# Splitting the next head's q and k at the head of a step, and a two-bank PSUM tile with a place of its own

## The chip, the cores and the metric

The kernel runs on one NeuronCore of one Trainium2 chip. The metric is the device time of one execution in microseconds (us). The engines named below are TensorE (PE in the rows, with its weight loads as PEld), VectorE (DVE), ScalarE (ACT), GpSimd (POOL) and SyncE (SP, which issues the DMAs here).

## What is computed

Causal attention with a monotone bias over 32 heads (4 x 8), 576 positions, 64 columns a head, then two MoE-like blocks on the 2304 tokens:

```python
scores = where(causal, -1e9, scale * q @ k.T + minimum(bias, 0))   # bias from a cumsum of max(s, 0)
x = softmax(scores) @ v                     # heads laid side by side: 2304 x 512
h = (x @ w1) * (x @ w2) @ w3                # 512 -> 1024 -> 1024
x = h @ w_out                               # 1024 -> 512
h = x @ w_in                                # 512 -> 1024
sm = softmax(h); solu = h * sm
ln = (solu - mean) / sqrt(var + 1e-6) * g_ln
out = ln @ w_out2                           # 1024 -> 512
```

## The kernel before

Most products are made from a high and a low word of each operand: ScalarE copies the operand into the rounded type (`hi`), an engine subtracts that from the operand (`lo`), and TensorE adds three products, high by high, high by low and low by high. The order of all instructions is set by a scheduler that goes through the program text and by the pools: an instruction waits for the buffer that its tile takes, and a tile takes the buffer that comes free first in its pool.

**Attention.** A loop over steps `st` (36 of them) issues for one head its scores (`qk_part`, parts 0 to 2: matmuls `sc`, lines 177 and 178, VectorE's masked maximum on line 186, ScalarE's exponential on line 190) and for the head two steps earlier the transposes (`tr`, line 247) and the products with v (`av`, line 275). The first 8 heads use unsplit q and k. From head 8 on `split_qk` splits them: ScalarE's `hi` of 64 x 1152 (line 93), a DMA that copies it (line 159), and GpSimd's `lo` (line 98). A step's head is split in the step before it, behind the transposes of that step.

Between these stand the units of the first MoE block as filler (`ab_unit`): 12 matmuls `a` = x·w1 (line 303), ScalarE's copy to `a_sb` (line 315), 12 matmuls `b` = x·w2, VectorE's product `g_sb` (line 323), which goes to DRAM (`g_scr`).

**Weights.** `pump` prepares weights, one job of 512 KB at a time. A job's DMA brings packed words into a `stage` buffer (2 buffers in the attention, 4 after it); ScalarE (line 340) and VectorE (lines 346, 347, 351) turn them into fp32; ScalarE makes the high word `W` (line 93) and VectorE the low word (line 98). The low word frees the stage buffer for the next DMA. 16 of these jobs, for w1 and w2, run in steps 3 to 16, beside the first units.

**PSUM.** It has eight banks. Up to step 10 a pool psA holds two tiles of two banks (`bigtile`, for the 576 columns of scores of a head's longest rows, the first matmul of part 0) and psB four of one bank (`smalltile`, for all the rest). At step 11 both are closed and replaced by psE, one tile of two banks, and psF, six of one bank. The first score tile of head 9 is the first that psE gives.

**M.** After the attention 16 jobs bring w3, and `m_unit(f)` makes the eight row blocks of M = w3·w_out (24 matmuls of 128x512, line 626). Its bank is a `smalltile`. The first comes right behind the last unit's `b`; the others follow in psD, four one-bank tiles of the pools that replace psE and psF. Then `x2_half` (`x`, line 710) multiplies g by M, `h_pair` computes h by seven products of halves in four banks with the tags X, Y, Z, W (psC), the softmax and the layer norm follow, and `out_unit(t)` computes the output tile of 128 rows: 24 matmuls of 128x512 (line 836), ScalarE's copy (line 841) and one DMA of 256 KB (line 842). There are 18 such tiles, and the last is the program's end.

Of the kernel before, what the change touches and what calls it, by code (L numbers as in the profile page):

```python
# [8 lines left out]
F32 = mybir.dt.float32  # L9
# [3 lines left out]
AF = mybir.ActivationFunctionType  # L13
ALU = mybir.AluOpType
AX = mybir.AxisListType
PSUM = bass.MemoryType.PSUM
# [10 lines left out]
def tile_attention_moe(  # L27
# [15 lines left out]
    nc = tc.nc  # L43
    B, H, D, _, S = qkT.shape
    NH = B * H
    T, DM = out.shape
# [3 lines left out]
    KF = DF // 128  # L50
# [6 lines left out]
    for i in (2, 3, 1, 4, 0):  # L57
# [3 lines left out]

    dram = ctx.enter_context(tc.tile_pool(name="dram", bufs=1, space=DRAM))
    ps_ctx = ExitStack()
    PSP = [
        ps_ctx.enter_context(tc.tile_pool(name="psA", bufs=2, space=PSUM)),
        ps_ctx.enter_context(tc.tile_pool(name="psB", bufs=4, space=PSUM)),
# [15 lines left out]
    def bigtile(name):  # L82
        return PSP[0].tile([128, 2, 512], F32, tag="A", name=name)

    def smalltile(name):
        return PSP[1].tile([128, 512], F32, tag="B", name=name)

    def flat(ap):
        return ap.rearrange("p a b -> p (a b)")
# [34 lines left out]
    def load_head(h):  # L124
        b, hh = divmod(h, H)
        if h < NQ:
            nc.sync.dma_start(out=QN[h % 3][64:128], in_=qkT[b, hh, :, 0])
            after[0] = nc.sync.dma_start(out=KN[h % 3][64:128], in_=qkT[b, hh, :, 1])
            return
        qk2 = at.tile([128, 2, S], F32, tag="qk2", bufs=2, name="qk2")  # L130
        after[0] = nc.sync.dma_start(
            out=qk2[64:128].rearrange("p a s -> p (a s)"), in_=qkT[b, hh].rearrange("d a s -> d (a s)"),
        )
        raw_t[h] = qk2[64:128]
# [18 lines left out]
    def split_qk(h):  # L153
        if h < NQ:
            return
        raw = raw_t.pop(h)
        t = QK[h % 2]
        hi(t[64:128, 0::2], raw)
        nc.sync.dma_start(out=t[0:64, 1:3].bitcast(F32), in_=t[64:128, 0::2].bitcast(F32))
        lo(t[64:128, 1::2], raw, t[64:128, 0::2], G)  # L160
# [36 lines left out]
    def qk_part(h, part):  # L197
        if part == 0:
            p_t[h] = at.tile([128, PW], F32, tag="P", bufs=PB, name="P")
        if part == 0:  # L200
            ps = flat(bigtile("sc"))
            qk_mm(h, [(0, ps[:, 512:1024]), (512, ps[:, 448:512])], 0)
            softmax_tile(h, 0, ps[:, 448:1024])
            return
        ps = smalltile("sc")
        o = 0
        views = []
        for ti in ((1, 4), (2, 3))[part - 1]:
            q0, rows, n, _ = QT[ti]
            qk_mm(h, [(0, ps[:, o:o + n])], ti)  # L210
            views.append((ti, ps[0:rows, o:o + n]))
            o += n
        for ti, view in views:
            softmax_tile(h, ti, view)
# [277 lines left out]
    for i in range(2):  # L492
# [14 lines left out]
        out=wmask[:, S - 128:S], in_=wmask[:, S - 128:S], pattern=[[-1, 128]],  # L507
# [36 lines left out]
    for st, (h, ph) in enumerate(steps):  # L544
        for _ in range(NF.get(st, 0)):
            fill.extend(ab_unit(*units.pop(0)))
        left = len(fill)
        if st == 11:
            ps_ctx.close()
            PSP[:] = [  # L550
                ps_ctx.enter_context(tc.tile_pool(name="psE", bufs=1, space=PSUM)),
                ps_ctx.enter_context(tc.tile_pool(name="psF", bufs=6, space=PSUM)),
            ]

        def F(share):
            while fill and len(fill) > left * (1 - share):
                fill.pop(0)()

        if h is not None:
            if NQ <= h + 2 < NH:  # L560
                load_head(h + 2)
            qk_part(h, 0)
        if st > 1:
            pump(PUMP.get(st, 0))
        if h is not None:
            qk_part(h, 1)
            qk_part(h, 2)
        F(FS)
        if h is not None:
            normalise(h)  # L570
        if ph is not None:
            for part in range(4):
                tr_part(ph, part)
        if late:
            with tc.issue_after(last_tr[0].ins):
                for fn in late.pop():
                    fn()
        if h is not None:
            if h % 2 == 1:
                load_v(h // 2)  # L580
            if NQ - 2 <= h < NQ:
                t = QK[h % 2] = at.tile([128, 4, S], F32R, tag="QK", bufs=2, name=f"QK{h % 2}")
                aug_rows(t[:, 0], t[:, 3])
            if h + 1 < NH:
                split_qk(h + 1)
            if h + 3 < NQ:
                load_head(h + 3)
                load_aug(h + 3, cumf_scr[h + 3:h + 4])
            if NQ <= h + 2 < NH:
                load_aug(h + 2, cum_scr[h + 2])  # L590
        F(1)
        if ph is not None and ph % 2:
            parts = av_parts(ph // 2)
            if ph < PD or st == len(steps) - 1:
                for fn in parts:
                    fn()
            else:
                late.append(parts)
# [4 lines left out]
    NT = T // 128  # L603
# [15 lines left out]
        w_job(w3L[f, :, 1024 * i:1024 * i + 1024], dst)  # L619

    def m_unit(f):
        ps = smalltile("m")
        for k in range(KF):
            H3, L3 = m_st[f, k // 4]
            for w_, o_ in ((H3, WOH), (H3, WOL), (L3, WOH)):
                nc.tensor.matmul(
                    ps, w_[:, k % 4], o_[:, k],
                    start=(k == 0 and w_ is H3 and o_ is WOH), stop=(k == KF - 1 and w_ is L3),
                )
        hi(MH[:, f], ps)  # L630
        lo(ML[:, f], ps, MH[:, f])
# [8 lines left out]
    for i in range(8):  # L640
# [8 lines left out]
    behind.clear()  # L649
    right0.close()  # L650
    ps_ctx.close()
    PSP[:] = [
        ctx.enter_context(tc.tile_pool(name="psC", bufs=1, space=PSUM)),
        ctx.enter_context(tc.tile_pool(name="psD", bufs=4, space=PSUM)),
    ]
    HD = DF // 2

    r2 = ctx.enter_context(tc.tile_pool(name="r2", bufs=1, side="right"))
# [39 lines left out]
    def x2_half(c, i):  # L698
        ps = smalltile("x2").rearrange("p (a t) -> p a t", a=2)
        x2_t[c, i] = ps  # L700
        last = None
        for a in range(2):
            m = 2 * i + a
            with ExitStack() as order:
                if last is not None:
                    order.enter_context(tc.issue_after(last.ins))
                for k in range(KF):
                    GH, GL = g_hl[c][k // 2]
                    for w_, g_ in ((MH, GH), (MH, GL), (ML, GH)):
                        last = nc.tensor.matmul(  # L710
                            ps[:, a], w_[:, k, m * 128:m * 128 + 128], g_[:, k % 2],
                            start=(k == 0 and w_ is MH and g_ is GH), stop=(k == KF - 1 and w_ is ML),
                        )
        if i == 1:
            g_hl.pop(c)
# [114 lines left out]

    def out_unit(t):
        LH, LL = lt_t.pop(t)
        ps = smalltile("o")
        for k in range(KF):
            for l_, w_ in ((LH, OH), (LH, OL), (LL, OH)):
                nc.tensor.matmul(  # L836
                    ps, l_[:, k], w_[:, k],
                    start=(k == 0 and l_ is LH and w_ is OH), stop=(k == KF - 1 and l_ is LL),
                )
        o = p2.tile([128, DM], F32, tag="o", bufs=1, name="o")  # L840
        nc.scalar.activation(out=o, in_=ps, func=AF.Copy)
        nc.sync.dma_start(out=out[t * 128:t * 128 + 128], in_=o)

    NCH = NT // 2

    def h_pair(c):
        t0, t1 = 2 * c, 2 * c + 1
        for t in (t0, t1):
            so = p2.tile([128, DF], F32, tag="so", bufs=2, name="so")
            ln_t[t] = so, p2.tile([128, 8], F32, tag="sv", bufs=4, name="sv")  # L850
        h0, h1 = ln_t[t0][0], ln_t[t1][0]
        X, Y, Z, W = (PSP[0].tile([128, HD], F32, tag=n, name=f"h{n}") for n in "XYZW")
        h_mm(X, "A11", "B11", True)
        copy(h0[:, 0:HD], X)
        h_mm(Z, "S1", "T1", True)
        copy(h1[:, HD:], Z)
        h_mm(Y, "A12", "B21", True)
        meet(t0, 0, Y)
        h_mm(X, "S2", "T2", False)
        copy(h0[:, HD:], X)  # L860
        if c + 1 < NCH:
            x2_first(c + 1)
        h_mm(Z, "S4", "B22", False)
        meet(t0, 1, Z)
        ln_exp(t0)
        h_mm(W, "A22", "T4", True)
        h_mm(X, "S3", "T3", False)
        copy(h1[:, 0:HD], X)
        ln_mean(t0)
        meet(t1, 1, X)  # L870
        meet(t1, 0, W)
        ln_exp(t1)
        ln_apply(t0)
# [34 lines left out]
    p2 = ctx.enter_context(tc.tile_pool(name="p2", bufs=1, side="left"))  # L908
    OH = p2.tile([128, KF, DM], F32R, name="OH")
    OL = p2.tile([128, KF, DM], F32R, name="OL")  # L910
    x2_half(0, 0)
    x2_first(0)
    x2_half(0, 1)
# [7 lines left out]
    for c in range(NCH):  # L921
# [8 lines left out]
        last = c == NCH - 1  # L930
# [77 lines left out]
```

## Time and profile before

| | us |
|---|---|
| median of 3 runs | 732.38 (731.66 to 733.02) |
| the profiled execution, its own time | 732.8 |
| its span, first to last instruction | 731.1 |
| TensorE busy | 714.2 |
| VectorE busy | 507.7 |
| ScalarE busy | 470.4 |
| GpSimd busy | 95.2 |

The span is what the rows cover; 1.7 us of the execution's own time lie outside it. The profiled execution is 0.4 us above the median, inside the range of the runs. A busy TensorE is one that has a matmul in flight; a matmul's row shows from its start to its modelled end, so that rows of consecutive matmuls overlap and the rate is read from their starts.

### The profile page before, as it was taken

The numbers are of one execution on the slowest core, as the hardware profiler recorded it, in microseconds if no ns is written. First come the engines' busy times: TensorE is split into PE (matmuls) and PEld (weight loads), VectorE is DVE, ScalarE is ACT, GpSimd is POOL, SyncE is SP. The second block draws the span as 40 slices with busy tenths as digits, with TensorE's granted clock in tenths as the row PEclk, the third lists the DMA queues.
The fourth block names the chain that finished last, engine by engine and source line by source line (L and its number), as shares of the span: only waits on it lengthen the run. The fifth ranks groups of instructions, "written<-read, shape, count | busy, mean of one in ns | idle before, by whom it ended". The sixth has DMA issues, their size and how long they took to land.

```text
span 731.1 us, 12896 instructions
## 1 busy us (share of the span) xinstructions
PE 714.2 (98%) x4618; PEld 631.5 (86%) x4618; DVE 507.7 (69%) x1251; ACT 470.4 (64%) x977; POOL 95.2 (13%) x88
## 2 busy tenths in 40 slices
PE   9989998999999999999998999999999999999997
PEld 6669888889899999999997889988888988888886
DVE  7996989898777887822777966675747366563651
ACT  7996878798676777822544735576737465563742
POOL 3051322234121221000000000001000000000000
PEclk9999999999999999999999999999999999999999
DMA  5644555555476655514566933153324252302311
GB/s 124 190 135 132 156 164 146 164 148 127 140 205 184 207 164 175 179 62 161 185 204 201 378 114 101 59 116 87 79 66 102 45 133 68 87 19 68 66 36 43
DMA packets 79827, 95.50 MB, mean 131 GB/s; under 512 B 41418, under 2 KB 52682, under 8 KB 79764
## 3 DMA queue, kind: packets, MB, share of 16 engines
q1 hardware_dynamic: 79764, 94.69, 44.5%
q8 instruction: 36, 0.59, 0.3%
q14 instruction: 27, 0.22, 0.1%
HBM read 59.04 MB, written 20.14 MB: 108 GB/s over the span
## 4 chain that ended last, share of the span: by engine, by line
PE 81%; DVE 9%; DMA 5%; ACT 2%; issue 2%; SPq 0%; DVEq 0%; ACTq 0%
PE x L710 14%; PE o L836 14%; PE a L303 12%; PE b L303 11%; PE av L275 6%; PE hX L742 5%; PE tr L247 5%; DMA stage<-in_w_dram 4%; PE hZ L742 3%; PE sc L178 2%; PE sc L177 2%; PE hW L742 2%; PE hY L742 2%; DVE stage L351 2%; PE sc L169 1%
## 5 line engine op out<-in xcount | busy, mean ns | idle before, releaser
L190 ACT ACTIVATE P<-P,STAT 64x64 f32<-64x64 f32 (+4 forms) x160 | 88.5, 556 | 22.9 <-DVE STAT L186 22.3
L98 POOL TENSOR_TENSOR QK<-qk,QK 64x1152 fp32r<-64x1152 f32 x24 | 66.2, 2759 | 172.9 <-ACT QK L93 172.8
L710 PE MATMUL x<-gl,MH 128*128 128x256 f32 x288 | 80.4, 279 | 0.0
L710 PE MATMUL x<-gh,ML 128*128 128x256 f32 x288 | 80.2, 279 | 0.0
L710 PE MATMUL x<-gh,MH 128*128 128x256 f32 x288 | 79.9, 279 | 0.0
L303 PE MATMUL b<-xT0h,W 128*128 128x288 f32 x256 | 58.4, 301 | 3.5 <-DVE W L98 2.1
L303 PE MATMUL a<-xT0h,W 128*128 128x288 f32 x256 | 59.2, 306 | 0.0
L247 PE MATMUL tr<-ident,P 128*128 128x128 f32 x416 | 54.4, 275 | 3.5 <-DVE STAT L186 2.7
L303 PE MATMUL a<-xT1h,W 128*128 128x288 f32 x256 | 57.6, 300 | 0.0
L836 PE MATMUL o<-OH,lh 128*128 128x512 f32 x144 | 57.0, 396 | 0.2 <-DVE ll L98 0.2
L836 PE MATMUL o<-OH,ll 128*128 128x512 f32 x144 | 57.0, 396 | 0.0
L836 PE MATMUL o<-OL,lh 128*128 128x512 f32 x144 | 57.0, 396 | 0.0
L303 PE MATMUL b<-xT1h,W 128*128 128x288 f32 x256 | 56.4, 295 | 0.0
L710 PEld LDWEIGHTS x<-gl,MH 128*128 128x128 f32 x288 | 54.1, 188 | 1.5 <-DVE gl L98 0.2
L710 PEld LDWEIGHTS x<-gh,MH 128*128 128x128 f32 x288 | 53.9, 188 | 1.1
L710 PEld LDWEIGHTS x<-gh,ML 128*128 128x128 f32 x288 | 54.0, 188 | 0.9
L806 DVE COPY lt<-turned 128x2048 uint16<-128x2048 uint16 x16 | 22.0, 1373 | 45.4 <-DMA turned<-half 45.4
L247 PEld LDWEIGHTS tr<-ident,P 128*128 128x128 f32 x416 | 46.8, 141 | 5.4 <-issue 1.6
L323 DVE TENSOR_TENSOR g_sb<-b,a_sb 128x288 f32<-128x288 f32 x64 | 28.7, 450 | 31.6 <-PE b L303 21.5
L340 ACT ACTIVATE stage<-stage 128x512 f32<-128x512 f32 x56 | 37.1, 679 | 20.5 <-DMA stage<-in_w_dram 18.7
L226 ACT ACTIVATE P<-P,STAT 128x576 f32<-128x576 f32 x64 | 42.7, 717 | 10.5 <-DVE STAT L219 10.4
L315 ACT ACTIVATE a_sb<-a 128x288 f32<-128x288 f32 x64 | 25.7, 403 | 36.3 <-PE a L303 36.0
(191 smaller groups left out, 1984.1 us busy)
## 6 DMA issues: line engine op xcount, KB each, us to landing
stage<-in_w_dram SPq DMA_DIRECT2D x32, 512.0 KB
g_scr<-g_sb SPq DMA_DIRECT2D x32, 288.0 KB
stage<-in_wo_dram SPq DMA_DIRECT2D x16, 512.0 KB
qk<-in_qk_dram SPq DMA_DIRECT2D x24, 288.0 KB
QK<-QK SPq DMA_DIRECT2D x24, 288.0 KB
gl<-g_scr SPq DMA_DIRECT2D x24, 256.0 KB
wf<-wf_scr SPq DMA_DIRECT2D x22, 256.0 KB
out_dram<-o SPq DMA_DIRECT2D x18, 256.0 KB
```

The costliest lines, as they stand in the source:

```text
L98: eng.tensor_tensor(out=dst, in0=src, in1=hi_.bitcast(F32), op=ALU.subtract)
L190: ex = nc.scalar.activation(out=dst, in_=dst, func=AF.Exp, bias=st[0:rows, ti:ti + 1], scale=-1.0, accum_out=st[0:rows, 5 + ti:6 + ti],)
L226: nc.scalar.activation(out=dst, in_=src, func=AF.Copy, scale=r)
L247: last_tr[0] = nc.tensor.transpose(ps[:, 128 * n:128 * n + 128], pt[:, o:o + 128], ident)
L275: nc.tensor.matmul(st["ps"][64 * e:64 * e + 64, 448 + c0:448 + c1], vr[:, j, e], PT[(2 * p + e) % 4][:, o + c0:o + c1], **kw,)
L303: nc.tensor.matmul(ps, w_[:, c, fs], x_[:, c, sl], start=(c == 0 and w_ is WH and x_ is XH), stop=(c == KC - 1 and w_ is WL),)
L315: ab_last[0] = nc.scalar.activation(out=a_sb, in_=ps, func=AF.Copy).ins
L323: ab_last[1] = nc.vector.tensor_tensor(out=g[:, sl], in0=ps, in1=st["a"], op=ALU.mult).ins
L340: nc.scalar.activation(out=high.bitcast(F32), in_=high.bitcast(F32), func=AF.Copy, scale=2.0 ** -112)
L710: last = nc.tensor.matmul(ps[:, a], w_[:, k, m * 128:m * 128 + 128], g_[:, k % 2], start=(k == 0 and w_ is MH and g_ is GH), stop=(k == KF ...
L742: last_h[0] = nc.tensor.matmul(ps, x_[:, k], w_[:, k], start=first and k == 0 and x_ is XH and w_ is WH, stop=k == 1 and x_ is XL, skip_gr ...
L836: nc.tensor.matmul(ps, l_[:, k], w_[:, k], start=(k == 0 and l_ is LH and w_ is OH), stop=(k == KF - 1 and l_ is LL),)
```

## The change

Four edits.

1. `split_qk(h + 1)` goes from behind the transposes of a step to the step's head, ahead of `qk_part(h, 0)` and of `pump`.
2. psE, the two-bank tile of step 11, is taken from the right side of PSUM, where psB's banks lay, and stays open past the end of the attention. Before, it lay on the left, where psA's lay.
3. M's first block takes that two-bank tile (its first bank) in place of a one-bank tile of psF. In `h_pair` the tags Z and W keep psC, X and Y get two banks in a new pool psG, which opens where psE lay, once psE is closed.
4. The last output tile is computed in two halves of 256 columns, each with 24 matmuls, a copy and a DMA of 128 KB, the second half's matmuls behind the first's.

```diff
         if st == 11:
             ps_ctx.close()
             PSP[:] = [
-                ps_ctx.enter_context(tc.tile_pool(name="psE", bufs=1, space=PSUM)),
+                big_ctx.enter_context(tc.tile_pool(name="psE", bufs=1, space=PSUM, side="right")),
                 ps_ctx.enter_context(tc.tile_pool(name="psF", bufs=6, space=PSUM)),
             ]
...
         if h is not None:
             if NQ <= h + 2 < NH:
                 load_head(h + 2)
+            if h + 1 < NH:
+                split_qk(h + 1)
             qk_part(h, 0)
...
-            if h + 1 < NH:
-                split_qk(h + 1)
             if h + 3 < NQ:
...
     def m_unit(f):
-        ps = smalltile("m")
+        ps = smalltile("m") if f else bigtile("m")[:, 0]
...
-    PSP[:] = [
-        ctx.enter_context(tc.tile_pool(name="psC", bufs=1, space=PSUM)),
-        ctx.enter_context(tc.tile_pool(name="psD", bufs=4, space=PSUM)),
-    ]
+    psp = {}
+    psp["Z"] = psp["W"] = ctx.enter_context(tc.tile_pool(name="psC", bufs=1, space=PSUM))
+    PSP[1] = ctx.enter_context(tc.tile_pool(name="psD", bufs=4, space=PSUM))
...
-        ps = smalltile("o")
-        for k in range(KF):
...
         o = p2.tile([128, DM], F32, tag="o", bufs=1, name="o")
-        nc.scalar.activation(out=o, in_=ps, func=AF.Copy)
-        nc.sync.dma_start(out=out[t * 128:t * 128 + 128], in_=o)
+        last = None
+        for c0, c1 in ((0, DM),) if t < NT - 1 else ((0, DM // 2), (DM // 2, DM)):
+            ps = smalltile("o")[:, 0:c1 - c0]
...
+            nc.scalar.activation(out=o[:, c0:c1], in_=ps, func=AF.Copy)
+            nc.sync.dma_start(out=out[t * 128:t * 128 + 128, c0:c1], in_=o[:, c0:c1])
...
+    big_ctx.close()
+    psp["X"] = psp["Y"] = ctx.enter_context(tc.tile_pool(name="psG", bufs=1, space=PSUM, side="right"))
```

The order of instructions moves only in some places: between head 9's first scores and the scores of head 15; where M passes into x; in the first `h_pair` calls; and in the last output tile. In all other places each engine has the same rows in the same order.

TensorE, at the first scores of head 9 (`QK_656`, in the change `QK_659`, is that head's split q and k), before:

```order
L303 MATMUL b<-xT0l,W_124 128x288
L303 MATMUL b<-xT0h,W_125 128x288
L177 MATMUL sc<-QK_656 128x512 [waits DMAHW0_49,DMAHW7_49,PE_49,Pool_49]
L178 MATMUL sc<-QK_656 128x512 [waits DMAHW1_49]
L177 MATMUL sc<-QK_656 128x64
L178 MATMUL sc<-QK_656 128x64
L303 MATMUL a<-xT0h,W_122 128x288 [waits Activation_49]
```

and with the change:

```order
L304 MATMUL b<-xT0h,W_124 128x288
L304 MATMUL b<-xT0l,W_124 128x288
L304 MATMUL b<-xT0h,W_125 128x288
L178 MATMUL sc<-QK_659 128x512 [waits DMAHW0_49,DMAHW7_49,DVE_49,Pool_49]
L179 MATMUL sc<-QK_659 128x512 [waits DMAHW1_49]
L178 MATMUL sc<-QK_659 128x64
L179 MATMUL sc<-QK_659 128x64
```

The scores now stand behind one more unit (12 `a` and 12 `b`) than before, and wait for VectorE, which reads the bank of that side last (a `g_sb`), in place of TensorE.

ScalarE, in the step of head 10 (`W02_124` is the high word of one weight job, `W00_122` of the next; `QK0_595` is head 10's split; P and STAT are the exponentials), before:

```order
L93 ACTIVATE QK1_656<-qk2_896 64x2x576
L190 ACTIVATE P_956,STAT2_118<-P_956,STAT2_118 128x576
L93 ACTIVATE W02_124<-stage_758 128x4x128
L93 ACTIVATE QK0_595<-qk2_954 64x2x576
L190 ACTIVATE P_898,STAT1_117<-P_898,STAT1_117 128x448
```

and with the change:

```order
L94 ACTIVATE P_959,STAT2_118<-P_959,STAT2_118 64x64
L94 ACTIVATE QK0_595<-qk2_954 64x2x576
L191 ACTIVATE P_959,STAT2_118<-P_959,STAT2_118 128x320
L316 ACTIVATE a_sb_1014<-a_1001 128x288
L191 ACTIVATE P_959,STAT2_118<-P_959,STAT2_118 128x192
L191 ACTIVATE P_959,STAT2_118<-P_959,STAT2_118 128x576
L94 ACTIVATE W02_124<-stage_761 128x4x128
L94 ACTIVATE W00_122<-stage_769 128x4x128
```

The first high word went behind head 10's split and behind the exponentials of two heads, and stands right ahead of the second.

VectorE, in the step of head 14 (`W_129` is the low word of a job; line 351, in the change 352, is the last step of a job's fp32 words, the one in front of `W_129` before being the next job's), before:

```order
L347 SCALAR_TENSOR_TENSOR stage<-stage 128x512
L228 TENSOR_SCALAR P<-P,STAT_116 64x64
L95 COPY PT_115<-tr 128x512
L95 COPY PT_115<-tr 64x3x64
L351 SCALAR_TENSOR_TENSOR stage<-stage 128x512
L98 TENSOR_TENSOR W_129<-stage,W_128 128x4x128
L186 ISA P,STAT_118<-sc,lmask 128x576
```

and with the change:

```order
L187 ISA P,STAT_118<-sc,lmask 128x576
L187 ISA STAT_118 128x1
L348 SCALAR_TENSOR_TENSOR stage<-stage 128x512
L96 COPY PT_115<-tr 128x128
L229 TENSOR_SCALAR P<-P,STAT_117 128x320
L229 TENSOR_SCALAR P<-P,STAT_117 128x192
L99 TENSOR_TENSOR W_129<-stage,W_128 128x4x128
L352 SCALAR_TENSOR_TENSOR stage<-stage 128x512
```

The low word now stands behind that head's first masked maximum and ahead of the next job's last step.

## Rows read from the trace of the kernel before

**Rows 1.** The page: busy time, share of the span and instructions.

```profile
PE 714.2 (98%) x4618; PEld 631.5 (86%) x4618; DVE 507.7 (69%) x1251; ACT 470.4 (64%) x977; POOL 95.2 (13%) x88
```

**Rows 2.** TensorE's waits from 60 to 160 us: total, times, longest.

```profile
PE b L303 <- DVE W L98: 2.1, 1, 2.1
PE tr L247 <- DVE STAT L186: 1.4, 1, 1.4
PE b L303 <- ACT W L93: 0.8, 1, 0.8
PE b L303 <- DVE g_sb L323: 0.7, 1, 0.7
PE sc L177 <- DVE g_sb L323: 0.3, 1, 0.3
```

**Rows 3.** Windows: PE, PEld, DVE, ACT, POOL busy, PEclk (granted clock), DMA share, GB/s.

```profile
80.00:100.00 20.00, 17.81 (x120) 16.71 (x120) 17.75 (x51) 16.37 (x48) 6.49 (x2) 0.91 0.60 178
120.00:140.00 20.00, 17.38 (x120) 15.64 (x121) 18.09 (x49) 15.08 (x35) 5.17 (x2) 0.91 0.65 187
160.00:350.00 190.00, 190.00 (x1453) 174.10 (x1452) 132.38 (x364) 123.66 (x303) 33.50 (x13) 1.00 0.52 158
```

**Rows 4.** VectorE's timeline from 79 to 124 us: start, duration, what.

```profile
79.97 3.14 DVE L98 TENSOR_TENSOR W<-stage,W 128x512 fp32r<-128x512 f32 x1
...
119.87 0.94 DVE L95 COPY PT<-tr 128x512 f32<-128x512 f32 x2
120.74 2.31 DVE L351 SCALAR_TENSOR_TENSOR stage<-stage 128x512 uint32<-128x512 uint32 x1
122.97 0.68 DVE L98 TENSOR_TENSOR W<-stage,W 128x512 fp32r<-128x512 f32 x1
```

**Rows 5.** GpSimd's timeline at 119 us.

```profile
119.86 2.64 POOL L98 TENSOR_TENSOR QK<-qk,QK 64x1152 fp32r<-64x1152 f32 x1 [5.71 <-ACT QK L93]
```

**Rows 6.** TensorE's timeline at 97 us.

```profile
97.67 0.30 PE L303 MATMUL b<-xT0h,W 128*128 128x288 f32 x1
```

**Rows 7.** ScalarE's timeline at 76 us and at 92 us.

```profile
76.87 0.67 ACT L93 ACTIVATE W<-stage 128x512 fp32r<-128x512 f32 x1
...
92.73 1.16 ACT L93 ACTIVATE QK<-qk 64x1152 fp32r<-64x1152 f32 x1
```

**Rows 8.** The chain of waits from 82 to 98 us: start, duration, what.

```profile
83.14 3.87 DMA stage<-in_w_dram
...
88.09 3.31 DMA stage<-in_w_dram
```

**Rows 9.** TensorE's waits from 380 to 440 us.

```profile
PE m L626 <- DVE g_sb L323: 2.2, 1, 2.2
PE m L626 <- ACT w3h L93: 0.6, 1, 0.6
```

**Rows 10.** The chain of waits from 427 to 429 us.

```profile
427.26 0.69 DVE stage L351
427.98 0.69 ACT w3h L93
```

**Rows 11.** Matmuls of x at 442 us, and the end of the last output tile.

```profile
441.83 0.28 PE L710 MATMUL x<-gl,MH 128*128 128x256 f32 x1
...
442.77 0.28 PE L710 MATMUL x<-gh,MH 128*128 128x256 f32 x1
...
726.68 0.40 PE L836 MATMUL o<-OL,lh 128*128 128x512 f32 x1
726.91 0.40 PE L836 MATMUL o<-OH,ll 128*128 128x512 f32 x1
727.40 0.60 ACT L841 ACTIVATE o<-o 128x512 f32<-128x512 f32 x1 [5.00 <-PE o L836]
```

**Rows 12.** ScalarE's copies of one shape, 60 to 300 us: busy, mean ns.

```profile
L93 ACT ACTIVATE PT<-tr 128x256 f32<-128x256 f32 x21 | 7.8, 372 | 0.0
```

**Rows 13.** DMA traffic from 727 to 731.1 us in 40 slices.

```profile
GB/s 0 0 0 0 0 0 0 0 0 0 0 0 0 0 0 0 0 0 360 380 340 380 380 440 240 40 0 0 0 0 0 0 0 0 0 0 0 0 0 0
```

More of the change, by code (lines that the diff above doesn't have):

```diff
@@ L63, in tile_attention_moe @@
     ps_ctx = ExitStack()
+    big_ctx = ExitStack()
     PSP = [
@@ L832, in out_unit @@
         LH, LL = lt_t.pop(t)
-        ps = smalltile("o")
-        for k in range(KF):
[L835 to L839, printed above, removed]
-        o = p2.tile([128, DM], F32, tag="o", bufs=1, name="o")
-        nc.scalar.activation(out=o, in_=ps, func=AF.Copy)
-        nc.sync.dma_start(out=out[t * 128:t * 128 + 128], in_=o)
+        o = p2.tile([128, DM], F32, tag="o", bufs=1, name="o")
+        last = None
+        for c0, c1 in ((0, DM),) if t < NT - 1 else ((0, DM // 2), (DM // 2, DM)):
+            ps = smalltile("o")[:, 0:c1 - c0]
+            with ExitStack() as order:
+                if last is not None:
+                    order.enter_context(tc.issue_after(last.ins))
+                for k in range(KF):
+                    for l_, w_ in ((LH, OH), (LH, OL), (LL, OH)):
+                        last = nc.tensor.matmul(
+                            ps, l_[:, k], w_[:, k, c0:c1],
+                            start=(k == 0 and l_ is LH and w_ is OH), stop=(k == KF - 1 and l_ is LL),
+                        )
+            nc.scalar.activation(out=o[:, c0:c1], in_=ps, func=AF.Copy)
+            nc.sync.dma_start(out=out[t * 128:t * 128 + 128, c0:c1], in_=o[:, c0:c1])
     NCH = NT // 2
@@ L851, in h_pair @@
         h0, h1 = ln_t[t0][0], ln_t[t1][0]
-        X, Y, Z, W = (PSP[0].tile([128, HD], F32, tag=n, name=f"h{n}") for n in "XYZW")
+        X, Y, Z, W = (psp[n].tile([128, HD], F32, tag=n, name=f"h{n}") for n in "XYZW")
         h_mm(X, "A11", "B11", True)
```

## Prediction, on record before the change was run

> **What bounds the kernel now.** I read the page first: TensorE has a matmul in flight in 98% of the span [rows 1], so a gain must come out of the 2% in which it has none, out of a lower clock, or out of the two ends of the program. The list of TensorE's waits says where the idle time lies: five waits between 60 and 160 us, 0.3 + 0.7 + 1.4 + 0.8 + 2.1 = 5.3 us [rows 2], and two at M, 2.2 and 0.6 us [rows 9]. The windows then show two things that the waits don't. From 160 to 350 us TensorE is busy for 190.00 of 190 us [rows 3], though heads are split there too, so the split as such costs nothing in that stretch. And in two windows, 80 to 100 and 120 to 140 us, the mean granted clock is 0.91 [rows 3]. As the clock has two levels, 1.2 and 2.4 GHz, 0.09 x 20 us = 1.8 us of full-speed work is lost in each. Each fall follows an idle spell of TensorE, of 1.4 us in the first window and of 0.8 and 2.1 us in the second. So the stretch from 70 to 130 us holds 5.3 + 2 x 1.8 = 8.9 us that could come back at most.
>
> The timelines name the causes. At 121.6 us a `b` unit waits for a low word `W`. VectorE stood in the next job's line 351, which took 2.31 us in place of 0.69 [rows 4, 10], and only then made the low word; GpSimd's `lo` of a head's q and k ran from 119.86 for 2.64 us [rows 5], the time in which that instruction was slow. At 79.97 us a low word itself took 3.14 us against the usual 0.68 [rows 4]; that one freed a stage buffer late, its DMA started at 83.14, the next job's at 88.09 and landed 3.31 us later, at 91.40 [rows 8], and VectorE stood at line 346 for it, ahead of a masked maximum that the transposes at 91 us waited for (the 1.4 us).
>
> **The change, part by part.** The trace shows none of the new order, so I walk it through: each instruction begins when its engine is free and what it waits for is done, with the duration of its row before.
>
> *PSUM tile on the right, split at the head (edits 1 and 2).* The same instructions run, in another order, from head 9's scores to head 15's.
> - Start: head 9's scores now wait for the third unit's `g_sb`, right behind that unit's last `b`. Such waits took 0.3 and 0.7 us [rows 2]; I give the new one 0.6 in place of the 0.3: +0.3.
> - The high word that ended at 77.5 us [rows 7] now stands behind head 10's split and the exponentials of heads 9 and 10. In the walk it comes at some 83.5. Its low word follows at 84 to 85, and the next job's at 86. So the stage loads start at some 84.7 and 86 in place of 83.14 and 88.09 [rows 8]; the first is late by 1.6 us, the second early by 2. By 3.3 to 3.9 us a load, stretched as two now run together, they land at about 89 and 91. What is late next is the following `b` unit, whose high word stands on ScalarE behind head 12's split, its exponentials and two copies: about 96.9. In the trace before that unit starts at 97.67 [rows 6], at half clock. So here the new order is 0.7 us ahead, the +0.3 counted in.
> - Around 120 us: the low word stands ahead of the next job's line 351, and the matmuls that need it stand later. In the walk the high word is ready at about 119, as TensorE gets there, and the low word at about 122, where TensorE needs it at 122.8. The waits of 0.8 and 2.1 us go, and with them the clock's fall: -4.7.
>
> That would be -5.4 at 130 us. Behind it the order is as before and TensorE has no wait to 350 us [rows 3], so what is gained there stays. But the walk takes every VectorE instruction at its usual length. GpSimd's `lo` is moved, not removed, and some VectorE instruction will run beside it. I take off one stretched low word, 3.14 - 0.68 = 2.46 [rows 4], and count -2.9. The bounds are -5.4 (nothing stretched that TensorE waits for; -8.9 if no other wait is left either) and the slower rival below. The split's ScalarE copy and its DMA are issued as often as before. On SP's queue the stage loads now stand behind the split's DMA and behind the next load of q and k, which waits for GpSimd's `lo` to free its buffer; in the walk GpSimd is done at about 84, just ahead of the low word that lets the stage load go, so I give this 0, and it would cost a `b` unit what GpSimd is later.
>
> The Trainium skill, GPSIMD Engine Reference, section Key points, says that GpSimd shares its SBUF interfaces with VectorE and that VectorE instructions with two SBUF inputs contend for them. The trace agrees: two copies out of PSUM took 0.94 us together beside the same GpSimd instruction that stretched line 351, which has two SBUF inputs, to 2.31 [rows 4, 5]. The rule speaks against the edit, since a move leaves the contention: by the rule alone the term would be near the upper end, by the walk alone -5.4.
>
> *M's first block in the two-bank tile (edit 3).* The first `m` waits 2.2 us for the last `g_sb` because it gets that product's bank [rows 9]. The two-bank tile is free since the last head's scores, and w_out's words and the first of w3's are made by then, or the wait would be for them; the wait goes. But M's blocks are fed by a chain of DMA, VectorE and ScalarE work that doesn't start from TensorE here: the words for a late block come at 427.98 + 0.69 = 428.67 us whatever TensorE does, where it waits 0.6 us already [rows 9, 10]. A TensorE that is 2.2 us earlier waits 2.8 there. What is left is the chain's own gain: VectorE's order has that job's line 351 (427.26 before [rows 10]) one instruction earlier, 0.6 us. I take -0.6; the ends are 0 and -2.2 (the chain moves up by all of it, as blocks that are read out earlier hold VectorE less).
>
> *psC and psG.* The same number of banks and users; TensorE has no wait in `h_pair`, and the changed order of the first pairs lies under its matmuls: 0. If a tag had to wait for psG's opening, it would cost at most one `h` product; I see no such wait in the order.
>
> *The last tile in halves (edit 4).* 48 matmuls of 256 columns for 24 of 512. By starts, x's 256 columns come each 0.94 / 8 = 0.118 us, and the output's 512 each 0.23 [rows 11]: 48 x 0.118 = 5.6 against 24 x 0.23 = 5.5, so 0 to +0.1. Behind the last matmul, the copy falls from 0.60 us [rows 11] to about the 0.37 of another copy of 128x256 [rows 12]: -0.23. The last DMA moves half: its bytes took 7 to 8 slices of 0.1 us [rows 13], so -0.35. The first half's copy and DMA lie under the second half's 2.8 us of matmuls. Together -0.5, between -0.2 (only the copy) and -0.6.
>
> Sum: -2.9 - 0.6 + 0 - 0.5 = -4.0 us. The profiled execution took 732.8, so 728.8; that execution lies 0.4 above the median, so I forecast 728.4 for the median.
>
> **The rivals.**
> - *All of it comes back.* No stretched instruction meets a low word that TensorE waits for, and M's chain moves up: -5.4 - 2.2 - 0.6 = -8.2, so 724.2. For it: the walk. Against it: VectorE is busy for 17.8 to 18.1 of 20 us there [rows 3], so little slack is left for any delay.
> - *The stalls only move.* The loads come no earlier in sum, a `b` unit still waits 2 to 3 us for its words, and the clock falls once more: the attention gives between 0 and -1, with M and the end 730.3 to 731.9. For it: the same work on the same full engines, 16 jobs through two stage buffers. Against it: the two waits before have named causes, and both causes are gone in the order.
> - *Slower: GpSimd's `lo` meets the low word at 97 us.* In the walk the high word there ends at 96.9, with no slack to the `b` that needs it, and the low word follows at once. GpSimd takes 2.64 us [rows 5]; if the head's split on ScalarE ends after 96.9 - 2.6 = 94.3 us, the low word runs beside it and takes 2.46 us longer, TensorE waits, and the clock falls as behind the other waits: 2.46 + 1.8 = 4.3. The next stage load leaves as much later, so that the wait around 120 us stays too. Then -0.7 + 4.3 - 0.6 - 0.5 = +2.5, so 734.9. For it: the split of that step ended at 92.73 + 1.16 = 93.9 before [rows 7], 0.4 us from there, and the walk's errors are of this size. Against it: the change issues the split ahead of what it stood behind.
>
> **How the numbers follow.** The forecast, within 1.8 us either way (726.6 to 730.2): 0.45. All comes back: 0.15. The stalls only move: 0.24. Slower: 0.16. The 80% range leaves out most of the slower case and the far end of the best one: 724.5 to 733.3. A measurement of this kernel tells 0.2%, 1.5 us, from no change, so faster means below 730.9. That takes the first two cases and a third of the third, 0.67; the rest of the third and a little of the slower one make 0.18 for the same; slower 0.15.
>
> **What the profile of the changed kernel would show.** Right: no wait of TensorE for a `W` low word over 1 us between 110 and 130 us, a granted clock of 1.0 in that window, the first `m` right behind the last `b`, a longer wait of `m` for `w3h` at M's end (some 2 us), and an end in which the last copy takes 0.37 us. Wrong: a `W` of line 99 that takes 2 us or more with a `b` behind it, a clock below 1 in a window from 80 to 130 us, or a gain at M that outlasts the last block. What would make the forecast wrong most is the first stretch, as its term is a difference of waits that each hang on half a microsecond.

## The result: 1% slower, and the profile after

| | us |
|---|---|
| before, median | 732.38 |
| the change, median of 5 runs | 740.08 (738.83 to 741.04) |
| ratio to before | 1.0098, 95% interval 1.0079 to 1.0118 |
| the change's profiled execution: its time, its span | 738.83, 737.1 |

The change is 7.2 us slower by the ratio; 728.4 was forecast. Where the time went is read from the first and last starts of TensorE's groups. Each column is the time from the end of the one to its left:

| us | first `a` to last `b` | to the last `m` | to the last `x` | to the last `o`'s end | to the span's end |
|---|---|---|---|---|---|
| before | 330.44 | 49.34 | 242.87 | 45.63 | 3.81 |
| the change | 337.01 | 48.49 | 243.34 | 45.71 | 3.25 |

All of the loss lies in the attention stretch, 6.6 us in these two executions, for which the forecast had -2.9. M and the end came near the forecast (-0.85 for -0.6, -0.5 for -0.5, the halves' matmuls counted in); `h` and x took 0.5 more where 0 was forecast.

TensorE's waits in the change from 60 to 160 us (answers to [rows 2]) and the windows (to [rows 3]):

```profile
PE b L304 <- DVE P L229: 3.8, 1, 3.8
PE tr L248 <- DVE g_sb L324: 3.2, 1, 3.2
PE b L304 <- ACT W L94: 1.6, 1, 1.6
PE sc L178 <- issue: 0.7, 1, 0.7
PE a L304 <- ACT PT L94: 0.5, 1, 0.5
PE a L304 <- ACT a_sb L316: 0.3, 1, 0.3
```

```profile
80.00:100.00 20.00, 15.69 (x106) 14.82 (x105) 17.24 (x37) 15.75 (x40) 6.87 (x3) 0.91 0.54 155
...
120.00:140.00 20.00, 16.78 (x109) 15.31 (x109) 17.19 (x45) 16.45 (x39) 5.29 (x2) 0.83 0.60 170
...
160.00:350.00 190.00, 189.94 (x1449) 173.64 (x1449) 132.09 (x370) 125.75 (x312) 34.63 (x13) 1.00 0.52 155
```

The waits add up to 10.1 us where they were 5.3, and the clock is at its lower level for longer: 0.09 and 0.17 of 20 us, 5.2 us lost, where it was 3.6. That is +4.8 and +1.6, 6.4 of the 6.6 us. From 160 us on TensorE is full again, as before.

VectorE's timeline in the change shows why (to [rows 4]); GpSimd's stands below it (to [rows 5]):

```profile
78.85 2.88 DVE L348 SCALAR_TENSOR_TENSOR stage<-stage 128x512 uint32<-128x512 uint32 x1
81.65 0.74 DVE L187 CUSTOM_DVE_ANT_0 P<-sc,lmask 128x576 f32<-128x576 f32 x1
...
82.33 3.74 DVE L352 SCALAR_TENSOR_TENSOR stage<-stage 128x512 uint32<-128x512 uint32 x2
...
86.94 0.69 DVE L96 COPY PT<-tr 128x512 f32<-128x512 f32 x1
...
97.67 2.83 DVE L348 SCALAR_TENSOR_TENSOR stage<-stage 128x512 uint32<-128x512 uint32 x1
...
113.83 0.74 DVE L187 CUSTOM_DVE_ANT_0 P<-sc,lmask 128x576 f32<-128x576 f32 x1
...
114.50 2.30 DVE L352 SCALAR_TENSOR_TENSOR stage<-stage 128x512 uint32<-128x512 uint32 x1
...
122.65 2.85 DVE L347 TENSOR_SCALAR stage<-stage 128x512 uint32<-128x512 uint32 x1 [1.40 <-DMA stage<-in_w_dram]
125.42 0.45 DVE L324 TENSOR_TENSOR g_sb<-b,a_sb 128x288 f32<-128x288 f32 x1
```

```profile
78.19 2.98 POOL L99 TENSOR_TENSOR QK<-qk,QK 64x1152 fp32r<-64x1152 f32 x1 [14.26 <-ACT QK L94]
82.48 3.04 POOL L99 TENSOR_TENSOR QK<-qk,QK 64x1152 fp32r<-64x1152 f32 x1 [1.31 <-ACT QK L94]
97.28 2.66 POOL L99 TENSOR_TENSOR QK<-qk,QK 64x1152 fp32r<-64x1152 f32 x1 [11.76 <-ACT QK L94]
113.56 2.69 POOL L99 TENSOR_TENSOR QK<-qk,QK 64x1152 fp32r<-64x1152 f32 x1 [13.62 <-ACT QK L94]
122.60 2.61 POOL L99 TENSOR_TENSOR QK<-qk,QK 64x1152 fp32r<-64x1152 f32 x1 [6.35 <-ACT QK L94]
```

Each of the five `lo` instructions of GpSimd catches one weight instruction of VectorE (lines 347, 348, 352; usually 0.4 to 0.7 us) and holds it to about its own end: 78.85 + 2.88 = 81.73 stands 0.56 behind GpSimd's 78.19 + 2.98 = 81.17. The five lose 10.8 us. Behind the held ones stand, in VectorE's order, the copy of the transposes at 86.94, the line 352 at 101.02 whose `W` a `b` waits 1.6 us for, and the `g_sb` at 125.42. TensorE waits 3.8 us behind the first and 3.2 behind the last, where VectorE had also stood 1.40 us for a stage load. For the wait of 3.8 us the profile names line 229, whose row ends no earlier than the `b` starts and which works on P in SBUF; that the copy in front of it freed the bank is argued from the order, and in the run with four pieces, below, the profile names the copy for the same `b`.

The hold itself is not new. Before, the same five low words held VectorE for 6.4 us in all: at 79.97 and 120.74 us [rows 4] and for less at three other places. GpSimd's row before the second of these three is also longer than its usual 2.65 us:

```profile
78.91 1.13 DVE L351 SCALAR_TENSOR_TENSOR stage<-stage 128x512 uint32<-128x512 uint32 x1
...
93.97 3.93 POOL L98 TENSOR_TENSOR QK<-qk,QK 64x1152 fp32r<-64x1152 f32 x1 [11.41 <-ACT QK L93]
...
96.95 1.51 DVE L351 SCALAR_TENSOR_TENSOR stage<-stage 128x512 uint32<-128x512 uint32 x1
...
113.00 1.18 DVE L218 TENSOR_SCALAR STAT<-STAT 128x5 f32<-128x5 f32 x1
```

So the new order adds 4.4 us of hold and puts it in front of other instructions; how much of the 6.6 us that makes is for the experiments.

At M the wait for the last `g_sb` is gone, and a part of it comes back as a longer wait for `w3h` (1.2 us, was 0.6); a wait of x for `gh` is new (to [rows 9]). ScalarE's last copy takes 0.38 us, was 0.60 (to [rows 11]):

```profile
PE m L627 <- ACT w3h L94: 1.2, 2, 0.9
PE x L710 <- ACT gh L94: 0.6, 1, 0.6
```

```profile
733.83 0.38 ACT L846 ACTIVATE o<-o 128x256 f32<-128x256 f32 x1 [2.40 <-PE o L842]
```

### The profile page after: what moved, and what is told of

Its sections match the earlier page's. It is cut to its first block, busy times and chain, and to the rows that moved or that the text cites. A ratio compares the mean times of both kernels' runs of the same rounds, so it can differ in the third digit from the quotient of the medians.

```text
span 737.1 us, 12955 instructions
## 1 busy us (share of the span) xinstructions
PE 716.9 (97%) x4642; PEld 634.1 (86%) x4642; DVE 511.2 (69%) x1251; ACT 470.9 (64%) x978; POOL 94.6 (13%) x88
## 4 chain that ended last, share of the span: by engine, by line
PE 75%; DVE 11%; DMA 6%; ACT 4%; issue 3%; SPq 0%; DVEq 0%; ACTq 0%
PE o L842 13%; PE x L710 13%; PE a L304 11%; PE b L304 10%; PE hX L742 5%; PE av L276 5%; PE tr L248 4%; DMA stage<-in_w_dram 4%; PE hZ L742 3%; PE sc L179 2%; DVE stage L352 2%; PE sc L178 2%; DVE P L187 2%; DVE stage L348 2%; PE hW L742 2%
## 5 line engine op out<-in xcount | busy, mean ns | idle before, releaser
L191 ACT ACTIVATE P<-P,STAT 128x576 f32<-128x576 f32 (+4 forms) x160 | 88.4, 554 | 25.7 <-DVE STAT L187 25.1
L304 PE MATMUL a<-xT0h,W 128*128 128x288 f32 x256 | 61.1, 310 | 0.8 <-ACT PT L94 0.5
L842 PE MATMUL o<-OH,lh 128*128 128x512 f32 (+1 forms) x152 | 58.4, 384 | 0.2 <-DVE ll L99 0.2
L842 PE MATMUL o<-OH,ll 128*128 128x512 f32 (+1 forms) x152 | 58.3, 383 | 0.0
L842 PE MATMUL o<-OL,lh 128*128 128x512 f32 (+1 forms) x152 | 58.3, 383 | 0.0
L276 PE MATMUL av<-PT,VT 128*64 128x64 f32 (+4 forms) x384 | 48.8, 394 | 0.0
```

The costliest lines, as they stand in the source:

```text
L191: ex = nc.scalar.activation(out=dst, in_=dst, func=AF.Exp, bias=st[0:rows, ti:ti + 1], scale=-1.0, accum_out=st[0:rows, 5 + ti:6 + ti],)
L276: nc.tensor.matmul(st["ps"][64 * e:64 * e + 64, 448 + c0:448 + c1], vr[:, j, e], PT[(2 * p + e) % 4][:, o + c0:o + c1], **kw,)
L304: nc.tensor.matmul(ps, w_[:, c, fs], x_[:, c, sl], start=(c == 0 and w_ is WH and x_ is XH), stop=(c == KC - 1 and w_ is WL),)
L842: last = nc.tensor.matmul(ps, l_[:, k], w_[:, k, c0:c1], start=(k == 0 and l_ is LH and w_ is OH), stop=(k == KF - 1 and l_ is LL),)
```

## The experiments

Ratios are to before, of runs on the same chip, with 95% intervals; 0.1% is 0.73 us.

| kernel | ratio | interval |
|---|---|---|
| edit 2 in the attention alone | 1.0118 | 1.0099 to 1.0136 |
| all but the tile's side | 1.0007 | 0.9995 to 1.0020 |
| halves of the last tile alone | 1.0000 | 0.9987 to 1.0012 |
| split at the head alone | 0.9999 | 0.9988 to 1.0010 |
| before, `lo` in 4 pieces | 0.9978 | 0.9961 to 0.9996 |
| the change, `lo` in 4 pieces | 1.0013 | 0.9987 to 1.0039 |
| the change, no `lo` of q and k | 0.9952 | 0.9937 to 0.9967 |
| before, no `lo` of q and k | 0.9924 | 0.9904 to 0.9944 |
| tile on the left, 4 pieces | 0.9978 | 0.9963 to 0.9994 |
| tile on the left, 8 pieces | 0.9957 | 0.9943 to 0.9971 |
| before, `lo` twice | 1.0502 | 1.0469 to 1.0534 |
| the change, 8 pieces | 1.0020 | 1.0005 to 1.0035 |
| the change, third unit in step 11 | 1.0095 | 1.0060 to 1.0131 |
| before, third unit in step 11 | 1.0032 | 1.0007 to 1.0057 |

**The edits apart.** Edit 2 without the rest:

```diff
-                ps_ctx.enter_context(tc.tile_pool(name="psE", bufs=1, space=PSUM)),
+                ps_ctx.enter_context(tc.tile_pool(name="psE", bufs=1, space=PSUM, side="right")),
```

> Edit 2 alone inside the attention: the two-bank tile on the right, closed with the other pools at the attention's end; the split, M, h and the last tile as before. The instructions of the attention stand as in the change, those behind it as before. Theory A (the tile's place alone reorders heads 9 to 15 and costs what the change lost there): the last b comes some 6.6 us later than before, the total is 6 to 7 us above before. Rival B (the split's move is part of the loss): less than 5 us above. Rival C (the loss needs the tile kept open past the attention): within 1 us of before.

It is 1.18% slower: the whole loss, and theory A. Its rows are the change's: the wait of 3.8 us and one of 2.9 stand there too.

The rest without the tile's side (the diff is against the change), with the pools psC and psD on the right instead and psG on the left:

```diff
-                big_ctx.enter_context(tc.tile_pool(name="psE", bufs=1, space=PSUM, side="right")),
+                big_ctx.enter_context(tc.tile_pool(name="psE", bufs=1, space=PSUM)),
...
-    psp["Z"] = psp["W"] = ctx.enter_context(tc.tile_pool(name="psC", bufs=1, space=PSUM))
-    PSP[1] = ctx.enter_context(tc.tile_pool(name="psD", bufs=4, space=PSUM))
+    psp["Z"] = psp["W"] = ctx.enter_context(tc.tile_pool(name="psC", bufs=1, space=PSUM, side="right"))
+    PSP[1] = ctx.enter_context(tc.tile_pool(name="psD", bufs=4, space=PSUM, side="right"))
...
-    psp["X"] = psp["Y"] = ctx.enter_context(tc.tile_pool(name="psG", bufs=1, space=PSUM, side="right"))
+    psp["X"] = psp["Y"] = ctx.enter_context(tc.tile_pool(name="psG", bufs=1, space=PSUM))
```

> Edits 1, 3 and 4 with the two-bank tile on the left, where it was before, and kept open; psC and psD open on the right in its stead. The attention's instructions stand as before, all behind it as in the change. Theory A: the attention takes as long as before, M gives 0.8, the tail 0.4, and the wait of x for gh in the first pairs takes 0.5 back or not: 0.7 to 1.3 us below before. Rival B (the split's move costs): above before by some us.

Even with before. TensorE's waits are nearly before's, number by number:

```profile
PE b L304 <- DVE W L99: 2.1, 1, 2.1
PE tr L248 <- DVE STAT L187: 1.4, 1, 1.4
PE b L304 <- ACT W L94: 0.7, 1, 0.7
PE b L304 <- DVE g_sb L324: 0.7, 1, 0.7
...
```

So the side of one tile is what the change paid for. The gain of 0.7 to 1.3 us that was expected doesn't show.

The halves alone (the diff of edit 4):

> Edit 4 alone, the last output tile in two halves. From the change's trace: the time from the last matmul's end to the program's end falls by 0.4 us, so 0.4 below before, hardly more than the interval. Rival: 48 matmuls of 256 columns are slower than 24 of 512 and take it back.

In the trace the time behind the last matmul falls from 3.8 to 3.3 us, but the timed runs, which scatter over 4.6 us, don't tell 0.4 from nothing.

The split's move alone (the diff of edit 1):

> Edit 1 alone, the split at the head of the step. All engines have the same instructions in the same order as before. Theory A: the same time, within 0.1%. Rival B: another time, if something but the order of instructions moves with it.

The same time. In the two traces the instructions stand in one order on every engine, so the split's new place in the text changed nothing that the chip runs.

**GpSimd's hold on VectorE.** The low words of q and k in four instructions, for both kernels:

```diff
-        lo(t[64:128, 1::2], raw, t[64:128, 0::2], G)
+        for i in range(4):
+            c = slice(144 * i, 144 * i + 144)
+            lo(t[64:128, 1::2, c], raw[:, :, c], t[64:128, 0::2, c], G)
```

> The kernel before with GpSimd's low words of a head's q and k made in four instructions of 64x288 in place of one of 64x1152. VectorE and TensorE keep their order. Theory A (a VectorE instruction with its operands in SBUF that begins beside GpSimd's waits until GpSimd's instruction ends, so VectorE's queue loses up to 2.5 us a head): the stretched instructions of 2.3 to 3.1 us fall to 1.3 us or less, the waits of TensorE for W at 120 us and for the maximum at 91 us shrink, 2 to 6 us below before. Rival B (bandwidth is shared in proportion, pieces change nothing): within 0.2%. Rival C (four starts make GpSimd's work longer): 1 to 3 us above.

> The change with the same four pieces. Theory A (the change lost its time because its order puts VectorE's instructions in SBUF beside GpSimd's): the stretched ones at 79, 83, 98, 114 and 123 us fall to 1.3 us or less, the waits of 3.8 and 3.2 us mostly go, and the total comes to 731 to 735, 5 to 9 us below the change. Rival B (the loss is the later place of head 9's scores and of the unit behind them): still 6 us or more above before.

Before gets 0.22% faster, and the change falls from 1.0098 to 1.0013, with wide runs (730.6 to 738.6). What lies between the two falls from 7.2 to 2.6 us, so 4.6 us (2.7 either way, by the intervals) go with the cut. The order hardly moves with it: to 380 us VectorE's is the same before, and in the change 11 of its 816 rows stand elsewhere. In the change's VectorE timeline the instruction that took 2.88 us takes 1.02, and the pair that took 3.74 takes 1.90:

```profile
78.93 1.02 DVE L350 SCALAR_TENSOR_TENSOR stage<-stage 128x512 uint32<-128x512 uint32 x1
...
80.55 1.90 DVE L354 SCALAR_TENSOR_TENSOR stage<-stage 128x512 uint32<-128x512 uint32 x2
```

Two waits of TensorE for the copy of the transposes are left in that trace:

```profile
PE a L306 <- DVE PT L96: 4.2, 1, 4.2
PE b L306 <- DVE PT L96: 1.2, 1, 1.2
...
```

The second is the wait that took 3.8 us in the change. The first stands at 124.66 us and is no hold: VectorE stood 4.24 us in front of that copy for a stage load, which was issued at 115.20 us, ahead of GpSimd's next low words, and landed 8.35 us later where others took 4 to 5. The profiled execution took 734.4 us, above the median of 732.3; whether such a load makes the wide runs isn't known.

The same two without those low words at all (the scores then lack the low words of q and k):

```diff
-        lo(t[64:128, 1::2], raw, t[64:128, 0::2], G)
...
                 aug_rows(t[:, 0], t[:, 3])
+                nc.gpsimd.memset(t[64:128, 1:4:2].bitcast(F32), 0.0)
```

> The change without GpSimd's low words of q and k (left out: they are set to zero once, so the scores lack the low words). No GpSimd instruction runs beside VectorE in the heads from 8 on. Theory A: no VectorE instruction over 1.2 us from 70 to 140 us, the total 5 us or more below the change. Rival B: within 3 us of the change.

> The kernel before, with the same low words left out. Theory A: the stretched instructions at 80 and 121 us go, 3 to 6 us below before, and the two kernels without low words differ by less than 3 us. Rival B: they differ by 6 us or more, as the full ones do.

Before falls by 0.76%, 5.6 us, the change from 1.0098 to 0.9952, 10.7 us. So leaving GpSimd's low words out gains before 5.6 us and the change 10.7, and of the 7.2 us between them 5.1 go (2.3 either way). These two runs change more than the hold: some 50 of VectorE's rows to 380 us stand elsewhere in each, as the scheduler made another order without the low words. A rest of 0.28%, 2.1 us, stays. Before without low words waits for little; the change keeps a wait of head 9's scores (0.7, no engine named) and waits for `W`, 1.2 us of them at the `b` that waited 3.8:

```profile
PE tr L246 <- DVE STAT L185: 1.5, 1, 1.5
PE sc L176 <- DVE PT L95: 0.2, 1, 0.2
```

```profile
PE b L303 <- ACT W L94: 1.8, 2, 1.2
PE sc L177 <- issue: 0.7, 1, 0.7
...
```

The opposite test, the low words computed twice:

```diff
         lo(t[64:128, 1::2], raw, t[64:128, 0::2], G)
+        lo(t[64:128, 1::2], raw, t[64:128, 0::2], G)
```

> The kernel before with GpSimd's low words of q and k computed twice, the second time over the first (no result changes). Theory A: a VectorE instruction that meets the pair waits up to 5 us, and what the low words cost (5.8 us by the runs without them) grows by half or more: 3 to 10 us above before. Rival B (GpSimd is off the path, VectorE isn't held): within 1 us of before.

5% slower, 37 us, far beyond the 10 that were the upper end. From 140 to 320 us, where TensorE was full, it is busy for 163.6 of 180, and VectorE, 140.2 before, for 157.5:

```profile
140.00:320.00 180.00, 163.60 (x1213) 144.79 (x1212) 157.51 (x361) 122.18 (x306) 86.74 (x32) 1.00 0.54 151
```

Before, the hold has cover there: 15 us of it fall between 160 and 350 us, where TensorE is full [rows 3]. Doubled, the cover is gone: TensorE stands idle for 16.4 us of the 180, and VectorE's rows have grown by 17.3. Of some 30 us of TensorE's waits to 380 us in that trace 27 name VectorE, none GpSimd. The direction is theory A's; this order too differs from before (89 of VectorE's rows).

**Versions to keep.** The tile on the left (as above), with four and with eight pieces (`range(8)`, slices of 72):

> The two-bank tile on the left (the attention's order of before), kept open for M's first block, the last tile in halves, and GpSimd's low words in four pieces. Theory A: the attention as in the kernel before with pieces, some 2.5 us shorter than before, the tail 0.45, M 0 to 0.4: 729.4 to 730.4. Rival: M's stage loses what pieces and halves give, as the runs with the tile on the left and with the halves alone came out even with before: 732 or more.

> The same with eight pieces of 64x144. Theory A in full (a VectorE instruction waits for the running piece alone): another 0 to 2 us below the four pieces. Rival (the start of each GpSimd instruction costs, and q and k come late for the scores): above the four pieces.

The four pieces give 0.22%, as on before; M, x and the halves add nothing that shows. The eight give 0.43%: 729.10 us, the fastest version that computes everything, 1.4% below the change by the ratios, and clear of before's noise. Its longest VectorE instruction of 128x512 beside GpSimd takes 1.0 us. GpSimd's own work grows with the pieces, its rows on `QK` from 72 us to 94 and 118.

**The rest.** The change with eight pieces:

> The change with GpSimd's low words in eight pieces. Theory A with a rest (GpSimd's hold on VectorE's queue is most of the loss; the place of head 9's scores behind one more unit and its words keep 2 to 3 us, as without any low words): 731 to 732.5, that is 2 to 3 us above the kernel with the tile on the left and eight pieces. If there is no such rest: 729 to 730. If pieces this small disorder the attention again: above 734.

Above the expected: 1.0020, 4.6 us over the tile on the left. TensorE waits there 3.9 us for `W` from ScalarE, 2.5 for a `g_sb` and 0.7 for GpSimd's low words themselves, so the rest is not a fixed 2 us; with 147 of VectorE's rows elsewhere it is another order as well. Last, the unit ahead of head 9's scores, with which the walk began, given to the next step, on the right and on the left:

```diff
-    NF = {10: 3, 11: 0, 12: 3,
+    NF = {10: 2, 11: 1, 12: 3,
```

> The change with the third unit given to step 11 in place of step 10, so that head 9's first scores stand behind two units as before, though their tile is on the right. If the unit ahead of head 9's scores is what sets off the loss (directly, and through what then meets GpSimd's low words): within 3 us of before. If the loss comes with any order but that of before (the meeting with GpSimd's low words is a matter of chance): 4 us or more above before.

> The control: the kernel before with the third unit given to step 11, the tile on the left. If the unit's step matters by itself: 2 us or more from before, and the run with the tile on the right is to be read against this one. If not: within 1.5 us of before.

The scores of head 9 then stand where they stood before, and it is still 0.95% slower with the tile on the right; on the left 0.32%. So the unit's place alone is not the cause. Nor does the amount of hold tell these two apart: from 70 to 130 us VectorE's rows beside GpSimd's low words run 7.7 us over their usual length in both traces (7.8 in before, the sixth low word counted in), and the right is 4.6 us slower than the left. With the tile on the right TensorE waits 3.6 us in two waits of scores where the profile names no engine, and for `g_sb`:

```profile
PE sc L178 <- issue: 3.6, 2, 2.2
PE b L304 <- DVE g_sb L324: 2.4, 1, 2.4
PE tr L248 <- DVE g_sb L324: 2.2, 2, 1.1
...
```

The right minus the left is 7.2 us with whole low words, 4.6 with the unit moved, 4.6 with eight pieces, 2.6 with four and 2.1 with none.

## Why the prediction was wrong

- **The step that failed** is the one on the walk to 130 us and the single stretched low word taken off it: "the walk takes every VectorE instruction at its usual length", and "I take off one stretched low word". The term was -2.9 and measured +6.6. The new order put five of VectorE's weight instructions beside GpSimd's five low words, held by 10.8 us in all, of which the walk priced 2.46. The two waits around 120 us did go, as the walk said, and the clock didn't follow (0.83 from 120 to 140 us): the `lo` that stood in front of them met other instructions, with the copy of the transposes and a `g_sb` behind them, for which TensorE waited longer. With the low words cut in four, at nearly the same order, 4.6 of the 7.2 us between the two kernels go.
- **What the walk left out.** It followed the high and low words to the `b` at 84 us. Its start was right: head 9's scores waited 0.67 us for the 0.6 given. Its high word came at 85.1 us, near the 83.5 of the walk. But that `b` also waits for a bank, by the order the one that VectorE's copy of the transposes frees, and that copy came at 87.6, behind 4.6 us of hold. A second wait on the same matmul decided. The low words, at 84 to 86 us in the walk, came at 89.3 and 90.4, and the `b` that was to start at 96.9 started at 102.4. Without hold the walk would still have been late: the `b` waits 1.2 us for its high word in the run without low words.
- **A row misread.** The unit at 97.67 us was taken "at half clock"; its matmuls start 0.13 us apart, against 0.24 up to 97.0 us, so the clock was back at its upper level by then.
- **The slower rival** had the mechanism, but one meeting, at the low word of 97 us, for +2.5. The mechanism came at other places, several times. Its chance of 0.16 was small for what the trace of before had: five held instructions in 50 us, two of them for more than 1.5 us, on an engine that is 90% busy in two of the windows [rows 3].
- **Edit 1** was walked through as if it moved the split. It moved nothing; that this edit doesn't do what it says could have been read from its order by itself, and then all effects in the attention belonged to the tile's side.
- **M**: right in the mechanism. The first `m` starts 0.13 us behind the last `b`'s start, and a part of the gain comes back at the later words, 0.6 us more for `w3h` where some 2 were expected. The size can't be settled: from the last `b` to the last `m` takes 47.6 to 49.7 us in the eight kernels with the edit, 48.5 in the change, and 48.3 to 51.4 in the eight without.
- **The last tile**: the trace's term was right, some 0.5 us behind the last matmul in each trace with the halves, too small for the runs. **`h`**: the 0 was off by 0.5 in the change, where x has a new wait for `gh` of 0.6; but kernels without the edit scatter by as much there (242.8 to 243.6 us).
- **Open** is what the tile's side costs beside GpSimd's hold: 2.1 us without low words, 2.6 with four pieces, 4.6 with eight. That the hold is the larger part is shown for four pieces and none, not for eight; and with the unit moved 4.6 us stay at equal hold. The waits of head 9's scores on the right (0.7 us, and 1.4 with the unit moved) are in the rows, but no run takes them away alone.

## What to carry to other kernels

Where a second engine shares a resource with the one that feeds TensorE, price every meeting that the new order makes, not one; a reordering that removes two named stalls leaves the cause in place and can move it. Look in the trace of before for every instruction that takes longer than its usual time, also where nobody waits for it yet. Read first from the order which edits move instructions at all. A long instruction of an engine off the path can be worth cutting into pieces: here three lines in place of one gave 0.22% with four pieces and 0.43% with eight, when the reordering cost 1%. And a run that leaves work out also gives the scheduler another order: compare the orders before the difference is put down to the work.

## What the runs showed of the hardware

- VectorE's held instruction waits rather than runs slower, by its end: in the traces of before and of the change 20 held instructions of 128x512 with two SBUF inputs end 0.55 to 0.56 us behind GpSimd's (81.73, 86.07, 100.50 and 116.80 us here, 123.05 in [rows 4]), a little less than their own usual 0.7, whatever time they began. What such an instruction loses is the rest of GpSimd's, up to 2.5 us here.
- It goes both ways: before, GpSimd's low word of 93.97 us took 3.93 us, 1.3 more than usual, while VectorE's lines 347 and 98 at 94.11 and 94.70 took their usual 0.67 and 0.68; the next one, at 96.95, was held and ended 0.56 behind GpSimd.
- Instructions of one SBUF input are held too (line 347, 2.85 us for 0.43; four such cases in the two traces end 0.29 behind GpSimd's), while those that read PSUM run through: the masked maximum at 113.83 us took its 0.74 inside GpSimd's 113.56 to 116.25. The Trainium skill, Advanced Engine Details and Errata, section VectorE Performance Modes, says that VectorE's second SBUF port is shared with GpSimd, and that GpSimd's instructions and those of VectorE in the modes with two read ports block each other. The trace agrees that they block each other, and gives the length; no row shows which mode line 347 ran in.
- Between pieces VectorE gets in: with four, its instruction of 128x512 took at most 1.3 us beside GpSimd, with eight at most 1.0.
